# Scores of two slots in one burst, and the first projection in items of 2x256 tokens with the odd tokens of four batches together

One core of one Trainium2 chip. The metric is the device time of one execution in microseconds; the core's span in the trace is some 1.8 us shorter.

## The reference

Attention of 8 batches x 8 heads x 576 tokens x 64 in which only scores within tau of the row's maximum count, followed by two projections with a gate between them.

```python
scores = scale * np.matmul(q, k.transpose(0, 1, 3, 2))
thresh = np.max(scores, axis=-1, keepdims=True) - tau
scores = np.where(scores >= thresh, scores, -1000000000.0)
attn = np.exp(scores - np.max(scores, axis=-1, keepdims=True))
attn = attn / (np.sum(attn, axis=-1, keepdims=True) + 1e-09)
x = np.matmul(attn, v)            # to (4608 tokens, 512)
h = x @ w_in                      # 512 -> 2048
g = h * np.clip(h + 3.0, 0.0, 6.0) / 6.0
return g @ w_out                  # 2048 -> 512
```

## The kernel before

The work is cut into 144 slots: 128 query rows of two heads, nine slots for four heads (a "quad"), 18 for a batch. In the traces here each engine executes its instructions in program order. A slot goes through the engines like this: scores on TensorE (PE) into PSUM; two copies with maximum on VectorE (DVE), "the maxima"; a bias on GpSimd (POOL); mask and exponential on ScalarE (ACT); reciprocal on DVE; normalising on POOL; transposing by DMA. Projections of an earlier batch are laid between: an "item" of the first projection (eight matmuls, a ReLU on ACT or DVE, a gate on DVE) and a "quarter" of a second-projection tile (four matmuls; after the fourth quarter DVE evicts the tile).

```python
for n, sl in enumerate(queue):
    ...                                     # exp of the slot before (ACT)
    sm_max(sl)                              # two maxima on DVE, then bias on POOL
    if slot != 8 and todo1:
        item, then = todo1.pop(0)
        h = mm1(item)                       # PE, in ps_h: two banks, one buffer
        r = mm1_relu(h, on_act=(slot in (0, 1, 3, 5)))
        mm1_gate(item, h, r)                # DVE
        ...
    ...                                     # reciprocal of the slot before (DVE)
    for _ in range(pieces):                 # one quarter in most slots
        if todo2:
            mm2_part(bb, mt, part)
            if part == 3:
                outs += mm2_out(bb, mt, on_act=False)   # eviction, DVE
    for i in range(2):
        sm_mask(sl, i)
    ...                                     # one job: a transpose, or attention x V
    if n + 1 < len(queue):
        queue[n + 1].tiles = scores(queue[n + 1].quad, queue[n + 1].slot)
    ...
# after the loop: the rest of the projections, with PSUM of the scores as well
```

A slot's scores fill four banks, and there is one such set: the next slot's scores wait for this slot's maxima.

## Time and profile before

| | before |
|---|---|
| median, us | 560.3 |
| span in the trace, us | 558.7 |
| start of slot 22's scores | 74.7 |
| start of slot 142's scores | 495.0 |
| from there to the end | 63.7 |
| a slot, mean of 120 | 3.50 |

From slot 22 on the projections run within the loop; the stretch up to slot 142 is the steady part, and what comes after it is called the end below. The page, the groups, the chain and the timeline of before are shown in the prediction.

### The profile page before, as it was taken

The numbers are of one execution on the slowest core, as the hardware profiler recorded it, in microseconds if no ns is written. First come the engines' busy times: TensorE is split into PE (matmuls) and PEld (weight loads), VectorE is DVE, ScalarE is ACT, GpSimd is POOL, SyncE is SP. The second block draws the span as 40 slices with busy tenths as digits, with TensorE's granted clock in tenths as the row PEclk, the third lists the DMA queues.
The fourth block names the chain that finished last, engine by engine and source line by source line (L and its number), as shares of the span: only waits on it lengthen the run. The fifth ranks groups of instructions, "written<-read, shape, count | busy, mean of one in ns | idle before, by whom it ended". The sixth has DMA issues, their size and how long they took to land.

```text
span 558.7 us, 11624 instructions
## 1 busy us (share of the span) xinstructions
PE 530.6 (95%) x3829; PEld 309.2 (55%) x3870; DVE 424.7 (76%) x1041; ACT 469.7 (84%) x999; POOL 305.3 (55%) x646
## 2 busy tenths in 40 slices
PE   8899798799999999999999999999999999999997
PEld 6655455555555555655555555655555565654663
DVE  3787686787878788887978788887978798883440
ACT  4899899798889999899898999899898999984440
POOL 2788878854556555755556555755556555561000
PEclk9999899999999999999999999999999999999999
DMA  5999979976789869978689889977689865454102
GB/s 121 137 120 173 196 128 190 204 142 126 137 158 152 152 136 157 178 149 146 130 148 152 173 131 160 175 147 147 131 145 166 150 144 114 100 109 94 38 20 76
DMA packets 286348, 77.52 MB, mean 139 GB/s; under 512 B 269264, under 2 KB 281808, under 8 KB 286288
## 3 DMA queue, kind: packets, MB, share of 16 engines
q1 hardware_dynamic: 267680, 67.47, 65.3%
q0 software_dynamic: 17408, 8.92, 13.6%
q8 instruction: 30, 0.49, 0.4%
q10 hardware_dynamic: 1200, 0.39, 0.3%
q14 instruction: 30, 0.25, 0.1%
HBM read 36.70 MB, written 9.44 MB: 83 GB/s over the span
## 4 chain that ended last, share of the span: by engine, by line
PE 55%; DVE 11%; ACT 8%; issue 4%; SPq 3%; DMA 2%; POOL 2%; DVEq 0%; POOLq 0%
PE h L357 17%; PE o L386 16%; PE s L260 15%; DVE s L281 5%; PE av L327 3%; ACT s L289 3%; ACT s L294 3%; DMA nq<-in_q_dram 2%; DVE g L374 2%; DVE r L368 2%; ACT r L366 1%; PE s L266 1%; PE tp L214 1%; SPq L310 1%; POOL pn L302 1%
## 5 line engine op out<-in xcount | busy, mean ns | idle before, releaser
L302 POOL TENSOR_SCALAR pn<-s,rinv 128x576 bf16<-128x576 f32 x288 | 211.6, 745 | 133.1 <-DVE rinv L297 57.3
L289 ACT ACTIVATE s<-s,bias 128x576 f32<-128x576 f32 x288 | 206.9, 766 | 36.3 <-POOL bias L284 35.2
L281 DVE TENSOR_SCALAR_CACHE_REDUCE s<-s 128x576 f32<-128x576 f32 x288 | 205.9, 752 | 40.3 <-PE s L260 29.9
L294 ACT ACTIVATE s<-s 128x576 f32<-128x576 f32 x288 | 192.7, 671 | 0.3
L260 PE MATMUL s<-kT,qT 64*128 64x288 f32 x1024 | 169.7, 430 | 5.1 <-DVE s L281 2.8
L357 PE MATMUL h<-xT,w_in_sb 128*128 128x320 bf16 (+1 forms) x1024 | 144.9, 287 | 5.9 <-DVE g L374 5.0
L386 PE MATMUL o<-w_out_sb,g 128*128 128x512 bf16 x535 | 133.5, 379 | 5.2 <-DVE osb L394 3.0
L357 PEld LDWEIGHTS <-w_in_sb 128*128 128x128 bf16 x1024 | 92.1, 97 | 68.9 <-issue 31.9
L374 DVE SCALAR_TENSOR_TENSOR g<-r,h 128x512 bf16<-128x512 f32 (+1 forms) x128 | 96.4, 755 | 41.7 <-ACT r L366 39.9
L260 PEld LDWEIGHTS s<-kT,qT 64*128 64x128 f32 x1024 | 93.7, 186 | 60.9 <-DVE s L281 24.0
L284 POOL TENSOR_SCALAR bias<-m 128x1 f32<-128x1 f32 x288 | 54.4, 189 | 66.6 <-DVE s L281 45.8
L386 PEld LDWEIGHTS <-g 128*128 128x128 bf16 x576 | 55.6, 98 | 57.4 <-issue 9.0
L366 ACT ACTIVATE r<-h,three 128x640 f32<-128x640 f32 (+1 forms) x74 | 54.4, 736 | 20.6 <-PE h L357 19.9
L294 ACT ACTIVATION_READ_ACCUMULATOR s<-s 128x1 f32 x288 | 54.2, 188 | 0.0
L368 DVE TENSOR_SCALAR r<-h 128x512 f32<-128x512 f32 (+1 forms) x54 | 40.5, 751 | 0.0
L394 DVE TENSOR_SCALAR osb<-o 128x512 f32<-128x512 f32 x31 | 21.0, 676 | 21.4 <-PE o L386 21.4
L327 PE MATMUL av<-pT,vm 128*64 128x512 bf16 x256 | 34.6, 393 | 2.0 <-ACT kT L204 2.0
L327 PEld LDWEIGHTS <-vm 128*64 128x64 bf16 x512 | 18.0, 111 | 25.3 <-issue 18.8
L297 DVE RECIPROCAL rinv<-rsum 128x2 f32<-128x2 f32 x144 | 23.0, 160 | 11.3 <-ACT s L294 10.5
L339 DVE CAST xT<-av 128x512 bf16<-128x512 f32 x32 | 21.8, 681 | 6.6 <-PE av L330 6.3
L281 DVE DVE_READ_ACCUMULATOR s<-s 128x1 f32 x288 | 23.9, 83 | 0.0
L266 PE MATMUL s<-kT,qT 64*64 64x288 f32 x256 | 20.1, 415 | 0.7 <-DVE s L281 0.7
(44 smaller groups left out, 241.4 us busy)
## 6 DMA issues: line engine op xcount, KB each, us to landing
km<-in_k_dram SPq DMA_DIRECT2D x64, 128.0 KB, 3.0
out_dram<-osb SPq DMA_DIRECT2D x31, 256.0 KB, 2.4
nq<-in_q_dram SPq DMA_DIRECT2D x96, 72.0 KB, 2.7
vm<-in_v_dram POOLq DMA_DIRECT2D x16, 256.0 KB, 5.6
w_in_sb<-in_moe_w_in_dram POOLq DMA_DIRECT2D x16, 128.0 KB, 4.3
w_out_sb<-in_moe_w_out_dram POOLq DMA_DIRECT2D x16, 128.0 KB, 4.5
pT<-pn SPq DMA_TRANSPOSE x119, 3.4
nq<-in_q_dram SPq DMA_DIRECT2D x14, 128.0 KB, 4.4
```

The source lines that it names most:

```text
L260: nc.tensor.matmul(tiles[a][:, hf, 0:HALF], qT_of(pair)[a * 64:(a + 1) * 64, t * P:(t + 1) * P], keys(pair, a, hf), start=True, stop=True)
L281: nc.vector.tensor_scalar(out=sl.s[:, i, :].rearrange("p (a b) -> p a b", a=2), in0=ps[:, :, 0:HALF], scalar1=1.0, scalar2=None, op0=Alu.m ...
L284: nc.gpsimd.tensor_scalar(out=sl.bias[:, i:i + 1], in0=sl.m[:, i:i + 1], scalar1=-scale, scalar2=tau, op0=Alu.mult, op1=Alu.add)
L289: nc.scalar.activation(out=s, in_=s, func=Act.Prelu, bias=sl.bias[:, i:i + 1], scale=scale, alpha=REJECT)
L294: nc.scalar.activation(out=s, in_=s, func=Act.Exp, accum_out=sl.rsum[:, i:i + 1])
L302: nc.gpsimd.tensor_scalar(out=pn[:, i, :], in0=sl.s[:, i, :], scalar1=sl.rinv[:, i:i + 1], scalar2=1.0, op0=Alu.mult, op1=Alu.mult)
L327: nc.tensor.matmul(ps[a * 64:(a + 1) * 64, :], vm[:, 2 * hp + a, c * D:(c + 1) * D], pT[:, 5 * a + c, cols], start=(c == 0), stop=False)
L357: nc.tensor.matmul(hps[:, n, 0:w], w_in_sb[:, ki, (ni + n) * P:(ni + n + 1) * P], xT[b][:, ki, c0:c0 + w], start=(ki == 0), stop=(ki == KI ...
L366: nc.scalar.activation(out=r, in_=hps, func=Act.Relu, bias=three[:])
L368: nc.vector.tensor_scalar(out=r, in0=hps, scalar1=3.0, scalar2=0.0, op0=Alu.add, op1=Alu.max)
L374: nc.vector.scalar_tensor_tensor(out=gbuf[:, ni:ni + 2, c0:c0 + w], in0=r, scalar=6.0, in1=hps, op0=Alu.min, op1=Alu.mult)
L386: nc.tensor.matmul(o_ps[0], gbuf[:, ni, mt * P:(mt + 1) * P], w_out_sb[:, ni, :], start=(ni == 0), stop=(ni == NI - 1))
```

## The change

The intent, as I read the code, is to spare PE the switch between the scores (fp32, 64-row tiles of the array) and the projections (bf16, the whole array) in every other slot. PSUM holds the scores of two slots in six banks; the even slot's tile has a large part (384 columns) in a bank of its own and a small part (192) in a bank that it shares with the odd slot. The attention products and transposes borrow the even slot's two large banks after its maxima. To make room, the first projection gets one bank (2x256 in place of up to 2x320), so the 64 odd tokens of each batch are collected for four batches. Quarters come two at a time in even slots; jobs that end on DVE come in odd slots.

```diff
+    def score_tile(n, a, rows=slice(0, P), k0=0, w=S):
+        c0 = 1536 * (1 - a) + (128 if lower(n) else 832) + k0
+        return ps_flat[rows, c0:c0 + w]
...
+    def scores(*ns):
+        parts = [(n, small) for n in reversed(ns) for small in (True, False)]
+        if len(ns) == 2 and all(n % NSLOT != 8 for n in ns):
+            parts.insert(0, parts.pop(2))
+        for n, small in parts:
+            score_part(n, small)
...
-        if slot != 8 and todo1:
-            item, then = todo1.pop(0)
+        if todo1 or todo3:
+            item, then = (todo1 or todo3).pop(0)
             h = mm1(item)
-            r = mm1_relu(h, on_act=(slot in (0, 1, 3, 5)))
+            r = mm1_relu(h, on_act=n % 2 == 0)
...
-        for _ in range(pieces):
+        for _ in range(0 if n % 2 else 2):
             if todo2:
...
+        elif quad % 2:
+            jobs = {0: ["q1", "av0late"], 1: ["k1"], 4: ["av1", "avr"], 5: ["alloc", "k0"], 6: ["q0"], 7: ["rest"],
+                    8: ["av0"]}
+        else:
+            jobs = {1: ["q1"], 2: ["k1"], 3: ["av1", "avr"], 4: ["alloc", "k0"], 5: ["q0"], 6: ["rest"]}
...
-        if n + 1 < len(queue):
-            queue[n + 1].tiles = scores(queue[n + 1].quad, queue[n + 1].slot)
+        if n + 1 < N1:
+            scores(n + 1)
+        elif n % 2 and n + 2 < len(queue):
+            scores(n + 1, n + 2)
```

More of the change, by code (lines that the diff above doesn't have):

```diff
@@ L43 @@
     N1 = 22
-    N2 = 28
+    HB = 6
+    OB = 7
     scale = 1.0 / math.sqrt(D)
+    M = 2 * 512
     tau = float(tau)
@@ L60 @@
     o_pool = ctx.enter_context(tc.tile_pool(name="op", bufs=3))
-    ps_s = ctx.enter_context(tc.psum_pool(name="ps_s", bufs=2))
-    ps_h = ctx.enter_context(tc.psum_pool(name="ps_h", bufs=1))
-    ps_o = ctx.enter_context(tc.psum_pool(name="ps_o", bufs=1))
-    ps_m = ctx.enter_context(tc.psum_pool(name="ps_m", bufs=1))
+    ps_pool = ctx.enter_context(tc.psum_pool(name="ps", bufs=1))
     ctx.enter_context(tc.manual_schedule())
+    ps = ps_pool.tile([P, 8, 512], F32, name="ps")
+    ps_flat = ps[:].rearrange("p b c -> p (b c)")
     nat = {}
@@ L73 @@
     xT = {}
+    xR = {}
     loads = []
@@ L162, in warm_up @@
     def warm_up(count):
-        warm = ps_h.tile([P, 2, 512], F32, tag="h", name="warm")
         for _ in range(count):
-            nc.tensor.transpose(warm[:, 0, 0:P], identf[:], identf[:])
+            nc.tensor.transpose(ps[:, 6, 0:P], identf[:], identf[:])
     warm_up(14)
@@ L171 @@
     nc.vector.memset(three[:], 3.0)
-    gbuf = g_pool.tile([P, NI, 2 * S], BF16, name="g")
+    gbuf = g_pool.tile([P, NI, M + 256], BF16, name="g")
     def alloc_qk(quad):
@@ L190, with burst, bank @@
     turn = 0
-    def bank(name):
+    def burst(n):
+        return n >= N1
+    def bank():
         nonlocal turn
         turn += 1
-        if now < N2 and turn % 2:
-            return ps_o.tile([P, 512], F32, tag="o", name=name)
-        return ps_m.tile([P, 512], F32, tag="m", name=name)
+        return ps[:, ((3, 0) if now < N1 else (5, 2))[turn % 2], :]
     def copy_out(out, in_):
@@ L208, in by_pe, with main_pe, transpose_q @@
         return pair // NPAIR < NB
-    def main_pe(src, pair):
-        ps = bank("tp")
+    def main_pe(src, pair, pb=None):
+        pb = bank() if pb is None else pb
         n = pair % 2
         for t in range(4):
-            nc.tensor.transpose(ps[:, t * P:(t + 1) * P], src[:, t, 2 * n:2 * n + 2, :], identf[:])
-        return ps
-    def transpose_q(pair):
+            nc.tensor.transpose(pb[:, t * P:(t + 1) * P], src[:, t, 2 * n:2 * n + 2, :], identf[:])
+        return pb
+    def transpose_q(pair, pb=None):
         nq = nat[pair // 2][0]
         if by_pe(pair):
-            ps = main_pe(nq[:, 0:1024].rearrange("p (t h d) -> p t h d", h=4, t=4), pair)
-            return lambda: nc.vector.tensor_copy(out=qT_of(pair)[:, 0:512], in_=ps[:])
+            pb = main_pe(nq[:, 0:1024].rearrange("p (t h d) -> p t h d", h=4, t=4), pair, pb)
+            return lambda: nc.vector.tensor_copy(out=qT_of(pair)[:, 0:512], in_=pb)
         n = pair % 2
         nc.vector.transpose(out=qT_of(pair), in_=nq[:, n * S:(n + 1) * S])
+        return lambda: None
     def transpose_k(pair):
-        ps = main_pe(nat[pair // 2][1], pair)
-        return lambda: copy_out(kT_of(pair)[:, 64:576], ps[:])
+        pb = main_pe(nat[pair // 2][1], pair)
+        return lambda: copy_out(kT_of(pair)[:, 64:576], pb)
     def transpose_rest(quad, of_k=True, of_q=True):
-        ps = bank("tr")
+        pb = bank()
         nq, _, kr = nat[quad]
@@ L233, in transpose_rest @@
         if of_k:
-            nc.tensor.transpose(ps[:, 0:P], kr[:], identf[:])
+            nc.tensor.transpose(pb[:, 0:P], kr[:], identf[:])
         if of_q:
-            nc.tensor.transpose(ps[:, P:2 * P], nq[:, 1024:1152], identf[:])
+            nc.tensor.transpose(pb[:, P:2 * P], nq[:, 1024:1152], identf[:])
         def evict():
             qT, kT = qkT[quad]
-            both = ps[:].rearrange("p (w n t) -> p w n t", n=2, t=64)
+            both = pb.rearrange("p (w n t) -> p w n t", n=2, t=64)
             if of_q:
@@ L246, in transpose_rest, with keys @@
         return evict
-    def keys(pair, a, hf):
-        kT = kT_of(pair)
-        c0 = 64 * (1 - a) + hf * HALF
-        return kT[a * 64:(a + 1) * 64, c0:c0 + HALF]
-    def scores(quad, slot):
-        tiles = [ps_s.tile([P, 2, 512], F32, tag="s", name="s") for _ in range(2)]
-        for hf in range(2):
-            if slot < 8:
-                pair, t = 2 * quad + slot // 4, slot % 4
-                for a in range(2):
-                    nc.tensor.matmul(tiles[a][:, hf, 0:HALF], qT_of(pair)[a * 64:(a + 1) * 64, t * P:(t + 1) * P],
-                                     keys(pair, a, hf), start=True, stop=True)
-            else:
-                for n in range(2):
-                    for a in range(2):
-                        pair = 2 * quad + n
-                        nc.tensor.matmul(tiles[a][n * 64:(n + 1) * 64, hf, 0:HALF],
-                                         qT_of(pair)[a * 64:(a + 1) * 64, 512:S], keys(pair, a, hf),
-                                         start=True, stop=True)
-        return tiles
+    def keys(pair, a, k0, w):
+        c0 = 64 * (1 - a) + k0
+        return kT_of(pair)[a * 64:(a + 1) * 64, c0:c0 + w]
@@ new lines, in score_tile, with lower, score_part @@
+    def score_tile(n, a, rows=slice(0, P), k0=0, w=S):
+        c0 = 1536 * (1 - a) + (128 if lower(n) else 832) + k0
+        return ps_flat[rows, c0:c0 + w]
+    def lower(n):
+        return burst(n) and n % 2
+    def score_part(n, small):
+        quad, slot = divmod(n, NSLOT)
+        k0, w = ((384, 192) if small else (0, 384)) if lower(n) else ((0, 192) if small else (192, 384))
+        if slot < 8:
+            pair, t = 2 * quad + slot // 4, slot % 4
+            for a in range(2):
+                nc.tensor.matmul(score_tile(n, a, k0=k0, w=w), qT_of(pair)[a * 64:(a + 1) * 64, t * P:(t + 1) * P],
+                                 keys(pair, a, k0, w), start=True, stop=True)
+        else:
+            for i in range(2):
+                for a in range(2):
+                    pair = 2 * quad + i
+                    nc.tensor.matmul(score_tile(n, a, rows=slice(i * 64, (i + 1) * 64), k0=k0, w=w),
+                                     qT_of(pair)[a * 64:(a + 1) * 64, 512:S], keys(pair, a, k0, w),
+                                     start=True, stop=True)
@@ L279, in sm_max @@
         sl.rinv = stat_pool.tile([P, 2], F32, tag="rinv", name="rinv")
-        for i, ps in enumerate(sl.tiles):
-            nc.vector.tensor_scalar(out=sl.s[:, i, :].rearrange("p (a b) -> p a b", a=2), in0=ps[:, :, 0:HALF],
+        for i in range(2):
+            nc.vector.tensor_scalar(out=sl.s[:, i, :], in0=score_tile(sl.n, i),
                                     scalar1=1.0, scalar2=None, op0=Alu.mult, op1=Alu.max,
@@ L313, in pe_transpose, with av @@
     def pe_transpose(sl):
-        ps = ps_h.tile([P, 2, 1024], BF16, tag="h", name="pt")
-        ps = ps[:].rearrange("p a b -> p (a b)")[:, 0:2 * S].rearrange("p (c t) -> p c t", t=P)
+        pb = ps_flat[:, 3072:3072 + S].bitcast(BF16).rearrange("p (c t) -> p c t", t=P)
         pn = sl.pn[:].rearrange("p a b -> p (a b)")
         for c in range(9):
-            nc.tensor.transpose(ps[:, c, :], pn[:, c * P:(c + 1) * P], identb[:])
-        return lambda: nc.vector.tensor_copy(out=sl.dst, in_=ps)
-    def av(ps, pair, pT, cols):
+            nc.tensor.transpose(pb[:, c, :], pn[:, c * P:(c + 1) * P], identb[:])
+        return lambda: nc.vector.tensor_copy(out=sl.dst, in_=pb)
+    def av(pb, pair, pT, cols):
         b, hp = divmod(pair, NPAIR)
@@ L326, in av @@
             for a in range(2):
-                nc.tensor.matmul(ps[a * 64:(a + 1) * 64, :], vm[:, 2 * hp + a, c * D:(c + 1) * D],
+                nc.tensor.matmul(pb[a * 64:(a + 1) * 64, :], vm[:, 2 * hp + a, c * D:(c + 1) * D],
                                  pT[:, 5 * a + c, cols], start=(c == 0), stop=False)
         for a in range(2):
-            nc.tensor.matmul(ps[a * 64:(a + 1) * 64, :], vr[:, a, hp, :], pT[:, 4, cols], start=False, stop=True)
+            nc.tensor.matmul(pb[a * 64:(a + 1) * 64, :], vr[:, a, hp, :], pT[:, 4, cols], start=False, stop=True)
     def av_main(pair):
@@ L334, in av_main, with mm1 @@
         if hp == 0:
-            xT[b] = x_pool.tile([P, KI, S], BF16, tag="xT", name="xT")
-        ps = bank("av")
-        av(ps[:], pair, pts[pair], slice(0, 512))
-        o0 = 64 if b % 2 else 0
-        nc.vector.tensor_copy(out=xT[b][:, hp, o0:o0 + 512], in_=ps[:])
+            xT[b] = x_pool.tile([P, KI, 512], BF16, tag="xT", name="xT")
+        pb = bank()
+        av(pb, pair, pts[pair], slice(0, 512))
+        nc.vector.tensor_copy(out=xT[b][:, hp, :], in_=pb)
     def av_rest(quad):
         b, g = divmod(quad, 2)
-        ps = bank("ar")
+        pb = bank()
         for n in range(2):
-            av(ps[:, n * 64:(n + 1) * 64], 2 * quad + n, ptr[quad], slice(n * 64, (n + 1) * 64))
-        o0 = 0 if b % 2 else 512
-        nc.vector.tensor_copy(out=xT[b][:, 2 * g:2 * g + 2, o0:o0 + 64],
-                              in_=ps[:, 0:P].rearrange("p (a b) -> p a b", a=2))
-    def mm1(item, pool=None):
-        b, ni, c0, w = item
-        hps = (pool or ps_h).tile([P, 2, 512], F32, tag="s" if pool else "h", name="h")
+            av(pb[:, n * 64:(n + 1) * 64], 2 * quad + n, ptr[quad], slice(n * 64, (n + 1) * 64))
+        if b % 4 == 0 and g == 0:
+            xR[b // 4] = x_pool.tile([P, KI, 256], BF16, tag="xR", name="xR")
+        o0 = 64 * (3 - b % 4)
+        nc.vector.tensor_copy(out=xR[b // 4][:, 2 * g:2 * g + 2, o0:o0 + 64],
+                              in_=pb[:, 0:P].rearrange("p (a b) -> p a b", a=2))
+    def mm1(item, hb=HB):
+        src, ni, c0, _ = item
+        hps = ps[:, hb, :].rearrange("p (n w) -> p n w", n=2)
         for n in range(2):
             for ki in range(KI):
-                nc.tensor.matmul(hps[:, n, 0:w], w_in_sb[:, ki, (ni + n) * P:(ni + n + 1) * P],
-                                 xT[b][:, ki, c0:c0 + w], start=(ki == 0), stop=(ki == KI - 1))
-        return hps[:, :, 0:w]
+                nc.tensor.matmul(hps[:, n, :], w_in_sb[:, ki, (ni + n) * P:(ni + n + 1) * P],
+                                 src[:, ki, c0:c0 + 256], start=(ki == 0), stop=(ki == KI - 1))
+        return hps
     def mm1_relu(hps, on_act):
-        w = hps.shape[2]
-        r = r_pool.tile([P, 2, 320], F32, tag="r", name="r")[:, :, 0:w]
+        r = r_pool.tile([P, 2, 256], F32, tag="r", name="r")[:]
         if on_act:
@@ L371, in mm1_gate, with mm2_part, mm2_out @@
     def mm1_gate(item, hps, r):
-        b, ni, c0, w = item
-        c0 += (b % 2) * S
-        nc.vector.scalar_tensor_tensor(out=gbuf[:, ni:ni + 2, c0:c0 + w], in0=r, scalar=6.0, in1=hps,
+        _, ni, _, g0 = item
+        nc.vector.scalar_tensor_tensor(out=gbuf[:, ni:ni + 2, g0:g0 + 256], in0=r, scalar=6.0, in1=hps,
                                        op0=Alu.min, op1=Alu.mult)
     o_ps = {}
-    def mm2_part(bb, mt, part, pool=None):
+    def mm2_part(b, t, part, ob=OB):
+        g0 = M + 64 * (3 - b % 4) if t == 4 else 512 * (b % 2) + P * t
         if part == 0:
-            if pool:
-                o_ps[0] = pool.tile([P, 2, 512], F32, tag="s", name="o")[:, 0, :]
-            else:
-                o_ps[0] = ps_o.tile([P, d_model], F32, tag="o", name="o")[:]
+            o_ps[0] = ps[:, ob, :]
         for ni in range(part * 4, part * 4 + 4):
-            nc.tensor.matmul(o_ps[0], gbuf[:, ni, mt * P:(mt + 1) * P], w_out_sb[:, ni, :],
+            nc.tensor.matmul(o_ps[0], gbuf[:, ni, g0:g0 + P], w_out_sb[:, ni, :],
                              start=(ni == 0), stop=(ni == NI - 1))
-    def mm2_out(bb, mt, on_act):
+    def mm2_out(b, t, on_act):
         osb = o_pool.tile([P, d_model], F32, tag="osb", name="osb")
@@ L394, in mm2_out @@
             nc.vector.tensor_scalar_mul(out=osb[:], in0=o_ps[0], scalar1=1.0 / 6.0)
-        b0 = 2 * bb * S
-        if mt == 4:
-            return [(osb[0:64, :], out[b0 + 512:b0 + S, :]), (osb[64:P, :], out[b0 + S + 512:b0 + 2 * S, :])]
-        r0, t = (b0, mt) if mt < 4 else (b0 + S, mt - 5)
-        return [(osb[:], out[r0 + t * P:r0 + (t + 1) * P, :])]
+        r0 = b * S + t * P
+        if t == 4:
+            return [(osb[0:64, :], out[r0:r0 + 64, :]), (osb[64:P, :], out[r0 - S:r0 - S + 64, :])]
+        return [(osb[:], out[r0:r0 + P, :])]
     todo1 = []
+    todo3 = []
     todo2 = []
@@ L412, in moe_of, with moe_of_rest @@
         items = []
-        for c0, w, mts in (((0, 320, (4, 5, 6)), (320, 256, (7, 8))) if b % 2 else
-                           ((0, 256, (0, 1)), (256, 320, (2, 3)))):
+        for c0 in (0, 256):
             for ni in range(0, NI, 2):
-                items.append(((b, ni, c0, w), ()))
-            items[-1] = (items[-1][0], [(b // 2, mt, part) for mt in mts for part in range(4)])
+                items.append(((xT[b], ni, c0, 512 * (b % 2) + c0), ()))
+            items[-1] = (items[-1][0], [(b, t, part) for t in (c0 // P, c0 // P + 1) for part in range(4)])
+        return items
+    def moe_of_rest(b):
+        items = [((xR[b // 4], ni, 0, M), ()) for ni in range(0, NI, 2)]
+        items[-1] = (items[-1][0], [(c, 4, part) for c in (b, b - 2) for part in range(4)])
         return items
@@ L432 @@
             sl = Slot()
-            sl.quad, sl.slot = quad, slot
+            sl.quad, sl.slot, sl.n = quad, slot, len(queue)
             sl.on_chip = len(queue) < N1 - 1 and len(queue) % 2 == 1
             queue.append(sl)
-    queue[0].tiles = scores(0, 0)
+    scores(0)
+    plan = []
+    for sl in queue:
+        quad, slot = sl.quad, sl.slot
+        if sl.n < N1:
+            jobs = {1 if quad else 2: ["q1"], 2 if quad else 3: ["k1"], 5: ["alloc", "q0"], 6: ["k0"], 7: ["rest"],
+                    8: ["av0"]}
+            if quad == 0:
+                jobs[1] = ["rest0"]
+            else:
+                jobs[3], jobs[4] = (["av1"], ["avr"]) if quad == 1 else (["av1", "avr"], [])
+        elif quad % 2:
+            jobs = {0: ["q1", "av0late"], 1: ["k1"], 4: ["av1", "avr"], 5: ["alloc", "k0"], 6: ["q0"], 7: ["rest"],
+                    8: ["av0"]}
+        else:
+            jobs = {1: ["q1"], 2: ["k1"], 3: ["av1", "avr"], 4: ["alloc", "k0"], 5: ["q0"], 6: ["rest"]}
+        if quad + 1 == NQUAD:
+            jobs = {s: [j for j in jobs[s] if j not in ("alloc", "k0", "q0", "rest")] for s in jobs}
+        plan.append(jobs.get(slot, []))
     prev = None
@@ L469 @@
         outs = []
-        pieces = 0 if slot == 3 else 1
-        if slot == 0:
-            second = True
-        if second and slot < 2 and len(todo2) > 1 and todo2[0][1] == todo2[1][1]:
-            pieces, second = 2, False
-        for _ in range(pieces):
+        for _ in range(0 if n % 2 else 2):
             if todo2:
-                bb, mt, part = todo2.pop(0)
-                mm2_part(bb, mt, part)
+                b2, t2, part = todo2.pop(0)
+                mm2_part(b2, t2, part)
@@ L481 @@
                 if part == 3:
-                    outs += mm2_out(bb, mt, on_act=False)
+                    outs += mm2_out(b2, t2, on_act=False)
         for i in range(2):
             sm_mask(sl, i)
-        evict = None
         nxt = 2 * quad + 2
-        if slot == (1 if quad else 2):
-            evict = transpose_q(2 * quad + 1)
-        elif slot == (2 if quad else 3):
-            evict = transpose_k(2 * quad + 1)
-        elif n == 1:
-            evict = transpose_rest(0, of_k=False)
-        elif slot == 3 and quad > 0:
-            av_main(2 * quad - 1)
-        elif slot == 4 and quad > 0:
-            av_rest(quad - 1)
-            if quad % 2 == 0:
-                todo1.extend(moe_of(quad // 2 - 1))
-        elif slot in (5, 6, 7) and quad + 1 < NQUAD:
-            if slot == 5:
-                alloc_qk(quad + 1)
-                evict = transpose_q(nxt)
-            elif slot == 6:
-                evict = transpose_k(nxt)
-            else:
-                evict = transpose_rest(quad + 1)
-        elif slot == 8:
-            av_main(2 * quad)
@@ L509 @@
-        if evict:
-            evict()
+        for job in plan[n]:
+            if job == "alloc":
+                alloc_qk(quad + 1)
+            elif job == "q1":
+                transpose_q(2 * quad + 1)()
+            elif job == "k1":
+                transpose_k(2 * quad + 1)()
+            elif job == "q0":
+                transpose_q(nxt)()
+            elif job == "k0":
+                transpose_k(nxt)()
+            elif job == "rest":
+                transpose_rest(quad + 1)()
+            elif job == "rest0":
+                transpose_rest(0, of_k=False)()
+            elif job == "av1":
+                av_main(2 * quad - 1)
+            elif job == "av0":
+                av_main(2 * quad)
+            elif job == "av0late":
+                av_main(2 * quad - 2)
+            elif job == "avr":
+                av_rest(quad - 1)
+                if quad % 2 == 0:
+                    todo1.extend(moe_of(quad // 2 - 1))
+                if quad % 8 == 0:
+                    todo3.extend(moe_of_rest(quad // 2 - 1))
@@ L534 @@
     last = NQUAD - 1
-    count = [1, 0]
+    count = [0, 0]
     def last_out():
@@ L546, in rest1 @@
     def rest1(item, then):
-        h = mm1(item, pool=ps_s if count[0] % 3 else None)
+        h = mm1(item, hb=count[0] % 6)
         count[0] += 1
@@ L553, in rest2 @@
         while todo2:
-            bb, mt, part = todo2.pop(0)
-            mm2_part(bb, mt, part, pool=ps_s if count[1] % 3 else None)
+            b2, t2, part = todo2.pop(0)
+            mm2_part(b2, t2, part, ob=6 + count[1] % 2)
             if part == 3:
                 flush()
-                if (bb, mt) == (B // 2 - 1, 8):
+                if (b2, t2) == (B - 1, 3):
                     last_out()
                 else:
-                    late.extend(mm2_out(bb, mt, on_act=(count[1] % 2 == 0)))
+                    late.extend(mm2_out(b2, t2, on_act=(count[1] % 2 == 0)))
                 count[1] += 1
-    for item in todo1:
+    for item in todo1 + todo3:
         rest1(*item)
@@ L568 @@
     av_rest(last)
-    for item in moe_of(B - 1):
+    for item in moe_of_rest(B - 1) + moe_of(B - 1):
         rest1(*item)
```

## The prediction

> **What bounds the kernel now.** I read the page first, then the groups by shape, then the chain of the work that ended last between 300 and 345 us, then the timeline of the same place.
>
> ```profile
> PE 530.6 (95%) x3829; PEld 309.2 (55%) x3870; DVE 424.7 (76%) x1041; ACT 469.7 (84%) x999; POOL 305.3 (55%) x646
> ...
> PE 55%; DVE 11%; ACT 8%; issue 4%; SPq 3%; DMA 2%; POOL 2%; DVEq 0%; POOLq 0%
> ```
>
> TensorE is busy 95% and holds 55% of the chain. Busy is not streaming, so I looked at a stretch of the chain (start us, us, what):
>
> ```profile
> 316.07 0.98 PE h L357 x8
> 317.05 0.05 issue
> 317.10 1.67 PE o L386 x7
> 318.77 1.17 PE s L260 x8
> 319.94 0.98 PE h L357 x8
> 320.92 0.86 PE o L386 x4
> 321.79 1.17 PE s L260 x8
> 322.96 0.98 PE h L357 x8
> ```
>
> A plain slot is scores 1.17, a 256-wide projection item 0.98, one quarter of a second-projection tile 0.86: 3.02 us with no wait, PE alone. Adding per 18 slots (one batch) 18 x 1.17 + 16 items x 1.085 (mean of 0.98 and 1.19) + 18 x 0.86 + four attention products of 1.19 + two small ones of 0.45 + four key transposes of 0.44 + two of 0.22 gives 61.8 us, or 3.43 a slot. Score starts in the trace, from slot 22 (74.7 us) to slot 142 (495.0 us), are 3.50 apart, and 3.49 in the later half. So the loop is TensorE bound with under 2% of waiting. After the last slot come some 60 us of projections alone.
>
> What the other engines do in a slot (busy us, mean ns of one):
>
> ```profile
> L281 DVE TENSOR_SCALAR_CACHE_REDUCE s<-s 128x576 f32<-128x576 f32 x288 | 205.9, 752 | 40.3 <-PE s L260 29.9 <-issue 3.0 <-POOL bias L284 2.6
> ...
> L374 DVE SCALAR_TENSOR_TENSOR g<-r,h 128x512 bf16<-128x512 f32 x64 | 44.0, 688 | 18.8 <-ACT r L366 17.9
> ...
> L366 ACT ACTIVATE r<-h,three 128x512 f32<-128x512 f32 x36 | 24.5, 682 | 5.2 <-PE h L357 5.0
> ...
> L394 DVE TENSOR_SCALAR osb<-o 128x512 f32<-128x512 f32 x31 | 21.0, 676 | 21.4 <-PE o L386 21.4
> ```
>
> Back to back these overlap by some 0.08 each: the timeline has the maxima 0.68 apart, and the gate's successor 0.60 after it. ACT needs about 3.1 us a slot, DVE 2.9.
>
> ```profile
> 303.33 0.75 DVE L281 TENSOR_SCALAR_CACHE_REDUCE s<-s 128x576 f32<-128x576 f32 x1
> ...
> 304.01 0.08 DVE L281 DVE_READ_ACCUMULATOR s<-s 128x1 f32 x1
> ...
> 304.29 0.79 PEld L260 LDWEIGHTS s<-kT,qT 64*128 64x128 f32 x8 [0.42 <-DVE s L281]
> 304.30 1.24 PE L260 MATMUL s<-kT,qT 64*128 64x288 f32 x8
> ```
>
> The last maximum ends at 304.09 and the next scores start 0.20 later: the hand-over that the change makes longer or shorter.
>
> **What the Trainium skill says.** "Trainium Kernel Development and Optimization", Performance Expectations: matmul busy time is a bad measure of distance from the roofline, as matmuls are pipelined. Agreed here: of the 3.02 us of a plain slot 2.70 stream. "TensorE: Matmul & The Clock Gate", Back-to-back issue gap: N/2.4 + 2.5 ns, so 109 and 216 ns at 256 and 512 columns; single records here start 108.5 and 216 ns apart. The same page, What happens when you issue a matmul: only weight loads are pulled ahead, matmuls stay in program order, so one waiting score matmul holds all behind it. The waits in this trace agree. "PSUM — Partial Sum Buffer", PSUM bank collisions: accesses are to be guarded by bank and quadrant, not by address. The built program agrees: the burst's first 192-wide matmul, which shares only a bank with the slot before, carries a wait on DVE.
>
> **The change, part by part.**
>
> *Removed on PE.* In single records a score group of four pass pairs starts at 304.295, its passes 0.242 apart, and the projection's first matmul starts at 305.563: 1.27, of which 0.97 streams, 0.105 is the first weight load and 0.195 the switch back. A burst of two slots pays the 0.30 once: 1.94 + 0.30 = 2.24 against 2.54. That is 0.15 a slot, or 18 us in 121 slots. The split into 192 and 384 columns streams as long as 288 twice. Projection columns are the same in number (144 items of 256 for 128 of 256 or 320), and each item's DVE work too.
>
> *Moved.* One pair of slots on PE is burst 2.24, item 0.87, two quarters 1.73, item 0.87 = 5.71 plus the jobs of that pair (0 to 2.09; 7.9 in nine pairs). If PE alone counted, nine pairs would take about 57.5 us against 62.8 measured for 18 slots now.
>
> *Added: a longer loop through DVE.* The order of instructions says that a burst waits for the odd slot's maxima, and on DVE there stand between burst and these: the even slot's maxima, its gate, a reciprocal, and in every second pair an output eviction. From the burst's start: its last matmul ends at 2.21 (drain 0.16 as recorded), maxima from 2.28 to 3.64; the item ends at 3.27, its ReLU on ACT runs 3.30 to 3.98, so the gate runs 4.00 to 4.60; reciprocal to 4.68; the odd maxima to 6.11 (0.68 + 0.75); hand-over 0.20: the next burst not before **6.33**. With an eviction: the two quarters stream until 4.84 and drain at 5.00, eviction 5.05 to 5.65, maxima to 7.08, next burst not before **7.28**. PE's 5.71 lies inside both; only pairs with many PE jobs outlast them.
>
> Nine pairs, by first slot modulo 18, the larger of PE and DVE; 0, 4, 8, 14 evict:
> 0: 7.28 (PE 5.71); 2: 7.80 (PE, keys and both attention products); 4: 7.28; 6: 6.33; 8: 7.28; 10: 6.33 (no second projection there); 12: 7.36 (PE); 14: 7.28; 16: 7.12 (PE). Sum 64.1, and about 1.2 more after pair 8, where the q transpose and the attention copy come after the odd gate on DVE and hold the burst's last part, which needs their bank. 65.3 for 18 slots, 3.63 a slot; about 1.7 less per batch before slot 76, where pair 2 has no items. Over slots 22 to 142 that is 427 us against 420.3 now: **+7**, although PE's own work shrank.
>
> *The end.* In the new order 30 items and 44 quarters follow the last burst; now it is 21 items and 34 quarters after the last scores. From slot 142's scores to the end: burst 2.2, 240 matmuls x 0.1087 = 26.1, 176 x 0.2165 = 38.1, attention 2.9, waits (last transposes, ReLU and gate) about 3, last eviction and store 4.1 = 76.4 against 558.7 - 495.0 = 63.7 now: **+12.7**. Less streams in the loop in exchange, but that only widens PE's waits if DVE's loop sets the pace.
>
> Sum: 560.5 + 7 + 12.7 = 580. Waits that I left out would add; pairs in which I have laid two waits in a row that in fact overlap would take off. I put 578.
>
> **The rivals.**
> 1. *PE stays the bound.* Loop 120 slots at about 3.15 to 3.2 and 12.7 more at the end: about 530 to 537. For it: PE is the bound now, and jobs were placed with care (DVE jobs only in odd slots, behind the burst). Against it: in six of nine pairs PE's own work is 0.4 to 1.9 us shorter than the DVE chain, and program order lets PE do nothing else meanwhile.
> 2. *DVE's loop, but evictions and the ReLU wait fall mostly beside PE-bound pairs*, about 3.5 a slot: the loop as now, the end longer: 570.
> 3. *ACT joins.* Its work per pair is 6.2, with a key copy 6.7, above 6.33; masks wait for a bias that stands behind two normalisations on POOL. If the ReLU then comes late, each pair grows by 0.2 to 0.4: 590.
> 4. *DMA.* Its share is 0.82 to 0.92 in the loop now; a loop no faster asks no more of it. I give it little.
>
> **Range and chances.** Rivals 2 and 3 bound the mechanism at 570 and 590. Rival 1, and the chance that someone who placed jobs so carefully had measured a gain, I give a sixth; it stretches the low side. 578, range 550 to 592. Faster by over 2% (below 549) 0.15, within 2% (to 572) 0.20, slower 0.65.
>
> **What would show it.** Right: score bursts of about 2.2 us, with idle time of PE or its weight load before their first matmul put down to the maxima on DVE, tens of us in total (24 + 2.8 now); idle time of DVE before the even maxima put down to scores; bursts 7.2 to 7.4 us apart where an eviction lies between, 6.3 to 6.5 in pairs without much PE work; PE's busy share in the loop below 93%; slot 142's scores near 502 us and 76 us after them. Wrong: bursts 5.7 to 6.2 us apart in pairs without jobs, which means that the maxima do not wait for the whole burst or that evictions come later; or a projection phase at the end of about 60 us.

## The result

| | before | after | predicted |
|---|---|---|---|
| median, us | 560.3 (559.6 to 561.2, 4 runs) | 581.7 (580.5 to 582.0, 4 runs) | 578 |
| ratio to before | | 1.0377 (1.0363 to 1.0392) | |
| slot 142's scores at | 495.0 | 502.7 | 502 |
| slots 22 to 142 | 420.3 | 428.1 | 427 |
| from there to the end | 63.7 | 77.6 | 76.4 |

The page after, busy time and the chain:

```profile
PE 535.2 (92%) x3998; PEld 328.2 (57%) x3998; DVE 424.2 (73%) x1060; ACT 473.6 (82%) x1012; POOL 305.3 (53%) x646
...
PE 45%; ACT 15%; DVE 13%; issue 7%; POOL 4%; DMA 3%; DVEq 0%; POOLq 0%
```

Only the weight loads got more work worth naming (PEld 309.2 to 328.2 us, off the bound); the share of every other engine fell, and PE holds 45% of the chain in place of 55%. The loop from 200 to 490 us, before and then after (us, then busy of PE, weight loads, DVE, ACT, POOL):

```profile
sum 290.00, PE 285.14 PEld 164.20 DVE 242.64 ACT 266.59 POOL 164.72; mean PE 95.05 PEld 54.73 DVE 80.88 ACT 88.86 POOL 54.91
```

```profile
sum 290.00, PE 274.69 PEld 168.25 DVE 233.05 ACT 259.24 POOL 160.77; mean PE 91.56 PEld 56.08 DVE 77.68 ACT 86.41 POOL 53.59
```

PE goes from 98.3% to 94.7%, and DVE, ACT and POOL are idler as well: a loop of waits, not a full engine. A pair with an eviction (slots 126 and 127, pair 0 of the table below) in the timeline after (start us, us, engine, line, operation; L269 scores, L372 and L397 projections, L380 ReLU, L296 maxima, L387 gate, L405 eviction):

```profile
446.36 2.21 PE L269 MATMUL ps<-kT,qT 64*128 64x192 f32 x16
...
448.50 1.05 PE L372 MATMUL ps<-xT,w_in_sb 128*128 128x256 bf16 x8
448.69 0.76 DVE L296 TENSOR_SCALAR_CACHE_REDUCE s<-ps 128x576 f32<-128x576 f32 x1 [1.33 <-PE ps L269]
...
449.38 1.89 PE L397 MATMUL ps<-w_out_sb,g 128*128 128x512 bf16 x8
...
449.58 0.69 ACT L380 ACTIVATE r<-ps,three 128x512 f32<-128x512 f32 x1 [0.47 <-PE ps L372]
...
450.31 0.69 DVE L387 SCALAR_TENSOR_TENSOR g<-r,ps 128x512 bf16<-128x512 f32 x1 [0.17 <-ACT r L380]
...
451.11 1.04 PE L372 MATMUL ps<-xT,w_in_sb 128*128 128x256 bf16 x8
451.31 0.69 DVE L405 TENSOR_SCALAR osb<-ps 128x512 f32<-128x512 f32 x1 [0.24 <-PE ps L397]
...
451.92 0.74 DVE L296 TENSOR_SCALAR_CACHE_REDUCE s<-ps 128x576 f32<-128x576 f32 x1
...
452.59 0.75 DVE L296 TENSOR_SCALAR_CACHE_REDUCE s<-ps 128x576 f32<-128x576 f32 x1
452.73 0.29 PEld L269 LDWEIGHTS ps<-kT,qT 64*128 64x128 f32 x2 [0.86 <-DVE s L296]
452.73 2.88 PE L269 MATMUL ps<-kT,qT 64*128 64x192 f32 x16 [0.58 <-DVE s L296]
```

The first burst takes 2.21 us and DVE stands idle for 1.33 us until it ends. Then the chain runs as the prediction has it: even maxima, gate behind ACT's ReLU, eviction behind the two quarters, odd maxima, and only then the next burst. The second burst shows how such waiting hides: from its first to its last matmul it takes 2.88 us, because the row half whose maximum was done at 452.7 starts and the other half starts 0.68 us later, one maximum. For 0.59 us of that time two matmuls of the first half alone count as PE busy, and only 0.09 us is idle. So I compare pairs by the start of the last matmul of each burst.

| pair (first slot modulo 18) | 0 | 2 | 4 | 6 | 8 | 10 | 12 | 14 | 16 | sum |
|---|---|---|---|---|---|---|---|---|---|---|
| predicted | 7.28 | 7.80 | 7.28 | 6.33 | 8.48 | 6.33 | 7.36 | 7.28 | 7.12 | 65.3 |
| after, median of 3 to 7 | 7.04 | 7.67 | 7.05 | 6.26 | 8.40 | 6.10 | 7.97 | 7.21 | 7.03 | 64.7 |

(The 8.48 holds the 1.2 us that the prediction put behind pair 8; pair 2 is taken from slot 92 on, where it has items.)

The end. The chain before, and then after (start us, us, what):

```profile
509.44 10.74 PE o L386 x49
...
521.65 15.72 PE h L357 x126
...
537.63 10.74 PE o L386 x49
...
548.42 6.22 PE o L386 x28
```

```profile
512.63 3.20 DMA pT<-pn
...
519.75 13.97 PE ps L397 x64
...
534.55 20.90 PE ps L372 x190
555.45 20.73 PE ps L397 x96
```

In these long pieces PE streams with hardly a gap before and after, only there is more left to do: 24 items in a row for 16, and 160 second-projection matmuls for 126 in these lines. After also waits 3.2 us for the last transposes, as predicted.

### The profile page after: what moved, and what is told of

It is laid out like the page before. It is cut to its first block, busy times and chain, and to the rows that moved or that the text cites. A ratio compares the mean times of both kernels' runs of the same rounds, so it can differ in the third digit from the quotient of the medians.

```text
span 580.2 us, 12005 instructions
## 1 busy us (share of the span) xinstructions
PE 535.2 (92%) x3998; PEld 328.2 (57%) x3998; DVE 424.2 (73%) x1060; ACT 473.6 (82%) x1012; POOL 305.3 (53%) x646
## 4 chain that ended last, share of the span: by engine, by line
PE 45%; ACT 15%; DVE 13%; issue 7%; POOL 4%; DMA 3%; DVEq 0%; POOLq 0%
PE ps L397 14%; PE ps L372 13%; PE ps L269 13%; DVE s L296 7%; ACT s L304 6%; ACT s L309 5%; ACT r L380 3%; PE ps L341 3%; POOL pn L317 3%; DMA w_out_sb<-in_moe_w_out_dram 2%; DVE g L387 1%; PE ps L275 1%; DVE r L382 1%; DVE xT L352 1%; DMA pR<-pn 1%
## 5 line engine op out<-in xcount | busy, mean ns | idle before, releaser
L296 DVE TENSOR_SCALAR_CACHE_REDUCE s<-ps 128x576 f32<-128x576 f32 x288 | 206.1, 751 | 58.3 <-PE ps L269 42.8
L269 PE MATMUL ps<-kT,qT 64*128 64x192 f32 (+1 forms) x1024 | 170.5, 424 | 11.7 <-DVE s L296 5.1
L372 PEld LDWEIGHTS <-w_in_sb 128*128 128x128 bf16 x1152 | 107.6, 98 | 69.2 <-issue 54.0
L372 PE MATMUL ps<-xT,w_in_sb 128*128 128x256 bf16 x1024 | 130.6, 273 | 16.0 <-DVE g L387 15.3
L397 PE MATMUL ps<-w_out_sb,g 128*128 128x512 bf16 x576 | 133.3, 379 | 1.5 <-DMA w_out_sb<-in_moe_w_out_dram 0.8
L269 PEld LDWEIGHTS ps<-kT,qT 64*128 64x128 f32 x1024 | 96.2, 186 | 57.9 <-DVE s L296 24.6
L387 DVE SCALAR_TENSOR_TENSOR g<-r,ps 128x512 bf16<-128x512 f32 x144 | 98.8, 687 | 37.2 <-ACT r L380 35.1
L397 PEld LDWEIGHTS <-g 128*128 128x128 bf16 x576 | 56.0, 98 | 59.5 <-issue 3.0
L380 ACT ACTIVATE r<-ps,three 128x512 f32<-128x512 f32 x86 | 58.7, 685 | 34.4 <-PE ps L372 33.8
L405 DVE TENSOR_SCALAR osb<-ps 128x512 f32<-128x512 f32 x30 | 20.6, 688 | 31.9 <-PE ps L397 31.9
L382 DVE TENSOR_SCALAR r<-ps 128x512 f32<-128x512 f32 x58 | 39.8, 686 | 0.6 <-PE ps L372 0.6
L341 PE MATMUL ps<-pT,vm 128*64 128x512 bf16 x256 | 34.6, 393 | 1.8 <-DMA pT<-pn 1.8
L275 PE MATMUL ps<-kT,qT 64*64 64x384 f32 (+1 forms) x256 | 23.4, 417 | 3.3 <-DVE s L296 1.3
```

What stands on the lines that cost most here:

```text
L269: nc.tensor.matmul(score_tile(n, a, k0=k0, w=w), qT_of(pair)[a * 64:(a + 1) * 64, t * P:(t + 1) * P], keys(pair, a, k0, w), start=True, st ...
L296: nc.vector.tensor_scalar(out=sl.s[:, i, :], in0=score_tile(sl.n, i), scalar1=1.0, scalar2=None, op0=Alu.mult, op1=Alu.max, accum_out=sl.m ...
L341: nc.tensor.matmul(pb[a * 64:(a + 1) * 64, :], vm[:, 2 * hp + a, c * D:(c + 1) * D], pT[:, 5 * a + c, cols], start=(c == 0), stop=False)
L372: nc.tensor.matmul(hps[:, n, :], w_in_sb[:, ki, (ni + n) * P:(ni + n + 1) * P], src[:, ki, c0:c0 + 256], start=(ki == 0), stop=(ki == KI - 1))
L380: nc.scalar.activation(out=r, in_=hps, func=Act.Relu, bias=three[:])
L382: nc.vector.tensor_scalar(out=r, in0=hps, scalar1=3.0, scalar2=0.0, op0=Alu.add, op1=Alu.max)
```

## The experiments

Names in bold are the runs' labels. "Loop" is the time from the last matmul of slot 22's scores (their burst, where there are bursts) to that of slot 142's: 420.3 before, 428.9 after.

**a_late_evict.** The eviction is held back until the odd maxima are issued.

```diff
+    held = []
...
         sm_max(sl)
+        outs = []
+        if held:
+            outs += mm2_out(*held.pop(), on_act=False)
...
-        outs = []
...
-                    outs += mm2_out(b2, t2, on_act=False)
+                    held.append((b2, t2))
```

> Only the output eviction on DVE moves: from between the even slot's gate and the odd slot's maxima to just behind the odd maxima. Theory (a burst waits for the odd maxima, and all that stands ahead of them on DVE is on the path): the four eviction pairs of nine fall from 7.04 us between burst ends to about 6.5, so 27 x 0.5 = 13 us less, 564 to 572 us in all. Rival (ACT's own work, or a bias late on POOL, sets the pace of the pairs): the same work in another order, at most 3 us less, 578 to 583.

Measured: 568.8 us, ratio 1.0143; loop 417.5. As expected. The eviction pairs 0, 4 and 14 went from 7.04, 7.05 and 7.21 to 6.10, 6.16 and 6.32; pair 8 stayed at 8.40, and pairs 6 and 16 grew by 0.48 and 0.14, which I did not trace. Timeline of pair 0 in this run (L405 eviction, L382 the odd slot's ReLU):

```profile
442.25 0.73 DVE L296 TENSOR_SCALAR_CACHE_REDUCE s<-ps 128x576 f32<-128x576 f32 x1
...
442.91 0.75 DVE L296 TENSOR_SCALAR_CACHE_REDUCE s<-ps 128x576 f32<-128x576 f32 x1
443.35 2.59 PE L269 MATMUL ps<-kT,qT 64*128 64x192 f32 x16
...
443.59 0.68 DVE L405 TENSOR_SCALAR osb<-ps 128x512 f32<-128x512 f32 x1
...
444.19 0.68 DVE L382 TENSOR_SCALAR r<-ps 128x512 f32<-128x512 f32 x1
```

The same work, moved behind the maxima, lies beside the burst. So the place of the eviction cost 11.4 us of loop, net of what pairs 6 and 16 lost: shown.

**b_single.** Bursts off, everything else as changed.

```diff
-        return n >= N1
+        return False
...
-        return ps[:, ((3, 0) if now < N1 else (5, 2))[turn % 2], :]
+        return ps[:, (3, 0)[turn % 2], :]
...
-        if n + 1 < N1:
-            scores(n + 1)
-        elif n % 2 and n + 2 < len(queue):
-            scores(n + 1, n + 2)
+        if n + 1 < len(queue):
+            scores(n + 1)
```

> The bursts alone are undone: one slot's scores at a time again, with the new projection items, the new jobs and the new places of the second projection kept. Theory: a score group then waits for one slot's maxima only and PE is the bound again: 57.5 + 9 x 0.3 = 60.2 us of PE work per 18 slots and a little waiting, about 3.4 a slot, 408 us for 120 slots, with 75 before and 77.5 behind: 558 to 566 us. Rival (the loss comes from the one bank of the projection, or from the second projection in even slots only): stays at 576 to 584.

Measured: 580.2 us, ratio 1.0345; loop 426.5. A miss: undoing the bursts alone gave nothing back. Its chain shows why (start us, us, what):

```profile
447.06 1.22 PE ps L269 x8
...
448.35 0.19 DVE s L296
...
449.04 0.76 DVE s L296 x3
449.80 0.61 DVE r L382
...
450.43 0.70 DVE g L387
...
451.18 1.03 PE ps L372 x8
```

After the odd slot's scores (447.06) PE has one item, but the chain goes through DVE: the odd maxima, for which the next scores wait, then the odd slot's ReLU and gate, for which the next item waits, since it needs the projection's one bank. The two waits end together: in the timeline those scores start at 449.17, are held up halfway for the second maximum and end at 451.08. With both quarters in even slots there is too little PE work in odd ones to cover 1.45 us of maxima.

**b2_single_quarter.** b_single with one quarter in every slot.

```diff
-        for _ in range(0 if n % 2 else 2):
+        for _ in range(1):
```

> As the run with one slot's scores at a time, which stayed at 580, but with one quarter of a second-projection tile in every slot in place of two in even slots. My explanation of that miss: with both quarters in even slots PE has only one item of 0.87 us (and jobs) between the odd slot's scores and the next ones, which wait for 1.45 us of odd maxima, and an eviction stands ahead of these, so DVE's chain paced there too. Then this run is PE bound, about 3.4 us a slot, 406 to 413 us for 120 slots, 558 to 565 in all. Rival (items of 256 in one bank, and the rest tokens of four batches together, cost the time): stays at 574 to 582.

Measured: 564.8 us, ratio 1.0075; loop 410.9, then 76.6 to the end. As expected: the new items in one bank, the rest tokens of four batches together and the new jobs cost under 1% in all: the loop is 9.4 us shorter than before, the end 12.9 us longer. Bursts, with both quarters in even slots, cost 18 us of loop on top (428.9 against 410.9). With one slot's scores at a time the quarters' place alone costs 15.6 of it (426.5 against 410.9), and bursts then add 2.3. Bursts with one quarter in every slot were not run, so what bursts alone cost stays open.

**c_relu_swap.** The even ReLU on DVE, the odd one on ACT.

```diff
-            r = mm1_relu(h, on_act=n % 2 == 0)
+            r = mm1_relu(h, on_act=n % 2 == 1)
```

> ReLU of even items on DVE and of odd ones on ACT, so as many as before on each, but now the even one stands ahead of the odd maxima on DVE: gate from 4.39 in place of 4.00 us after the burst's start. Theory: 0.39 x about 40 pairs that DVE's chain paces, 594 to 602 us. Rival (throughput of ACT or of DVE paces): no work is added, 579 to 585.

Measured: 592.7 us, ratio 1.0570; loop 439.0, so 10.1 more with no work added. A little less than expected: in pairs 0 and 10 nothing changed (7.04 and 6.11), in pairs 4, 6 and 14 it added 0.12 to 0.22, and nearly all of it fell on pairs 16 (0.88) and 2 (0.56), which the prediction had put down to PE. In an eviction pair the later gate can hide in the wait for the quarters (0.24 us idle ahead of the eviction above). In pair 16 the trace shows another path than the odd maxima: the odd gate now waits for ACT, the attention copy stands behind it, and the burst that begins at 387.84 waits in its last part for that copy's bank:

```profile
388.33 0.69 DVE L387 SCALAR_TENSOR_TENSOR g<-r,ps 128x512 bf16<-128x512 f32 x1 [1.29 <-ACT r L380]
...
389.01 0.67 DVE L352 CAST xT<-ps 128x512 bf16<-128x512 f32 x1
...
389.74 0.29 PEld L269 LDWEIGHTS ps<-kT,qT 64*128 64x128 f32 x2 [0.31 <-DVE xT L352]
```

This burst spans 2.81 us where in the changed kernel it spans 2.21: 0.60 of the 0.88. Pair 2 I did not trace. So the run speaks against throughput as the pace, as no work was added, but it is no proof of the step through the odd maxima.

**g_dve_extra** and **h_act_extra.** One idle instruction more in each even slot from 22 on, on one engine. In the trace of g_dve_extra the memset takes 272 ns, in that of h_act_extra the copy 284 ns (285 in the trace of k_f1_act_extra), 61 of each.

```diff
+        if n >= N1 and n % 2 == 0:
+            nc.vector.memset(scratch[:], 0.0)          # g_dve_extra, ahead of the masks
         for i in range(2):
             sm_mask(sl, i)
+        if n >= N1 and n % 2 == 0:
+            nc.scalar.copy(out=scratch2[:], in_=scratch[:])   # h_act_extra
```

> A memset of 128x256 on DVE (some 0.2 us of pace) is added in even slots from 22 on, ahead of the odd maxima: 61 times. Theory (DVE's chain paces six of nine pairs): 0.2 x 40 = 8, so 587 to 593 us. Rival (ACT or PE paces): 580 to 584.

> A copy of 128x128 on ACT (some 0.2 to 0.25 us of pace) is added behind the masks of even slots from 22 on, 61 times, with nothing else changed. Theory (DVE's chain paces; ACT has 6.2 us of work in a pair of 7.1): at most 3 us more, 581 to 585 us. Rival (ACT paces, as its 90% of the loop and its 15% of the chain say): 0.22 x 61 = 13, so 593 to 597 us.

Measured: 590.5 us (ratio 1.0529) with DVE's, 584.2 us (ratio 1.0411) with ACT's. The profiled execution of h_act_extra took 2881 us; the three others, 583.2 to 584.3, are used, and nothing is read from its timeline but the copy's length. Nearly equal work costs 8.8 us on DVE ahead of the odd maxima and 2.4 us on ACT. The trace of g_dve_extra says where: pairs 0, 4, 6, 8, 10 and 14, the six in which the prediction had DVE's chain outlast PE, grew by 0.22 or 0.23 each, pairs 2 and 16 not at all, and pair 12 fell by 0.17. So DVE's chain paces these six, and ACT, though 15% of the chain, hardly does.

**d_even_first.** Where the odd slot before a burst used neither of the two large banks, the burst starts with the even slot.

```diff
+        if len(ns) == 2 and free_banks(ns[0] - 1):
+            parts = [(ns[0], False), (ns[0], True), (ns[1], True), (ns[1], False)]
...
```

> The burst's order alone changes where the odd slot before it left the two big score banks free (five of nine pairs): the even slot's large part first, which needs no maxima of the odd slot, then its small part, then the odd slot. The even maxima can then begin about 1 us earlier. Theory: pairs behind such a burst lose 0.7 to 1.0 us, 33 of them, so 549 to 560 us. Rival (the score matmuls' waiting is not what paces): 576 to 583.

Measured: 575.2 us, ratio 1.0261; loop 420.8. A miss: just below the rival's range and far from the theory's. The direction is right, the size (8.0 us of loop) about a third of what I expected: pairs 0, 4 and 14 lost 0.65, pair 10 0.33 and pair 6 0.14, but pairs 8 and 12 grew by 0.35.

**e_both.** a_late_evict and d_even_first together.

> Both mends together: output eviction behind the odd maxima, and the even slot first in the burst where its banks are free. Theory: most pairs come near PE's own work, 3.25 to 3.35 us a slot, 390 to 402 us for 120 slots, and with 75 before and 77.5 behind 543 to 555 us, faster than both kernels. Rival: not below 565.

Measured: 570.0 us, ratio 1.0171; loop 417.1. A miss, the rival's range: with the late eviction the even-first order adds nothing (417.5 without it). What pairs 0, 6 and 10 gain, pairs 8 and 12 lose again.

**f1_late_av_first.** a_late_evict, and the attention copy ahead of the q transpose in pair 8.

```diff
-            jobs = {0: ["q1", "av0late"], 1: ["k1"],
+            jobs = {0: ["av0late", "q1"], 1: ["k1"],
```

> The run with the late eviction, and in pair 8 of nine the attention copy on DVE ahead of the q transpose, so that the bank which the burst's last part needs is free some 0.7 us earlier. Theory (that pair's 8.4 us in place of 7.3 comes from this order): 0.7 x 6 or 7 = 4 to 5 us off 568.8, so 563 to 566. Rival (something else, such as V's loads issued on POOL there, makes the pair long): 567 to 570.

Measured: 565.5 us, ratio 1.0079; loop 412.3. As expected. Pair 8 went from 8.40 to 7.74 and no other pair moved by over 0.01: the order of two DVE instructions, through a bank, is worth 5.2 us of loop.

**f2_all_swap.** e_both, the attention copy first and the ReLUs swapped.

> Late eviction, even slot first in the burst where it can be, attention copy first, and the even ReLU on DVE with the odd one on ACT. With both mends the trace shows the even gate waiting 1 to 2.4 us for ACT's ReLU, which stands behind two exponentials, so ACT's order has become what paces. If so this goes to 552 to 562 us. If DVE's own chain still paces, the swap adds as it did alone, and it stays at 568 to 580.

Measured: 580.9 us, ratio 1.0349; loop 427.4. The reading that ACT's order had become what paces falls: the loop is 10.3 longer than in e_both, though the attention copy comes first. What the swap costs here by itself no run shows; if the copy's place is worth 5.2 as in f1_late_av_first, it is more than the 10.1 that it cost alone.

**k_f1_act_extra** and **l_f1_dve_extra.** The idle instructions of above on top of f1_late_av_first.

> The copy of 0.284 us on ACT in 61 even slots, now on top of the kernel with the late eviction and the attention copy first (565.5 us). Where it was added to the changed kernel it cost 2.4 us. My guess of what paces after the mend: ACT, whose own work per pair (6.2 us) is now close to the pair's 6.1 to 6.7. If so, 8 to 14 us more, 573 to 580. If PE or DVE's chain paces there too: 565 to 569.

> The memset of 0.272 us on DVE in 61 even slots, on top of the same mended kernel. In the changed kernel it cost 8.8 us. If ACT paces after the mend, at most 4 us, 565 to 569; if DVE's chain still does, 572 to 576.

Measured: 567.0 us (ratio 1.0122) with ACT's, 572.1 us (ratio 1.0202) with DVE's; f1_late_av_first has 1.0079. My guess fell again: ACT's costs 0.4%, DVE's 1.2%. By pairs (medians, as in the table), DVE's adds 0.17 to 0.23 in pairs 0, 4, 10 and 14, 0.06 in pair 6 and nothing in 2, 8 and 16; ACT's adds 0.19 in pair 8 and 0.02 or less elsewhere. After both mends DVE's chain still sets the pace of four of nine pairs; there the 0.30 us of switching that a burst saves on PE cannot show. No version beat the kernel before.

## Why the prediction was right

**The bound before** held: PE busy for 98% of the loop.

**The loop.** Predicted +7 us, measured +7.8. The step that carries it, "a burst waits for the odd slot's maxima, and on DVE there stand ... its gate, a reciprocal, and in every second pair an output eviction", is shown by two runs that shorten or lengthen just that chain: eviction taken off it (0.9 us less in pairs 0, 4 and 14, 11.4 us of loop), a memset of 0.27 us put on it (0.22 more in each of the six pairs that the prediction gave to DVE, 8.8 us in all). The swapped ReLUs (+10.1) are no third proof: they cost most in two other pairs. The nine pair times agree within 0.24 us, but for one.

**The sum** is nearer than its parts. Six batches of 65.3, pairs 4 to 14 once more (43.1) and three times 1.7 off give 430 us, not the recorded 427: +9.5, not +7. The parts were some 0.6 a batch too long, so that the loop's agreement within 1 us is in part luck. (By its own steps 6.33 should read 6.31.)

**That one is pair 12**: 7.36 predicted as PE's own work, 7.97 in four of seven cases, 8.39 and 9.05 in two. In the chain a load of V issued on POOL comes ahead of the bias; these lines are of the case of 8.39, and the same order stands in the cases of 7.97:

```profile
424.42 0.70 POOL vm L125
...
425.31 0.19 POOL bias L299
...
425.53 1.44 ACT s L304 x2
```

That is the third rival's mechanism, a bias late on POOL, in one pair of nine. The chain goes on through mask, exponential, ReLU and gate to the odd item, which needs the projection's one bank and waits for the gate, some 0.57 us in the cases of 7.97 and 1.00 in that of 8.39: a path that the prediction did not have. The seventh case, slot 138, lies in the last batch, where no V is left to load, and took 7.44. No run moved that load, so this points to it and does not show it.

**Pair 8's 1.2 us**, "the q transpose and the attention copy come after the odd gate on DVE and hold the burst's last part", is right: exchanging the two gave 0.66 us of it back, with the late eviction in place.

**The end.** Predicted +12.7 us, measured +13.8: 30 items and 44 quarters behind the last burst for 21 and 34, by the order of the instructions, at the same rate of streaming (second projection: 10.74 us for 49 matmuls before, 13.97 for 64 after). Behind slot 142's first score PE was busy for 70.7 us in place of 58.3; these 12.4 us of PE work left the loop and did not make it shorter.

**What was off.** PE's busy share was to fall "below 93%" in the loop; it is 94.7%, in part because one row half's matmuls count as busy while the other half waits (0.59 us in the burst above), and the waits of the score's weight loads for the maxima grew only from 26.8 to 32.9 us in all. Bursts "7.2 to 7.4 us apart where an eviction lies between" come near for the ends of bursts (7.04 to 7.21, pair 8 apart), not for their starts (6.37), as one row half starts a maximum early; "6.3 to 6.5 in pairs without much PE work" came out as 6.26 and 6.10. That early start was not in my hand-over of 0.20 us; the pairs paced by DVE came out 0.07 to 0.24 us too long.

**A point that the prediction did not make**: it laid the loss on the burst. b_single shows that the single-slot form loses as much with the quarters where they are; what the two have in common, by their chains, is that between two groups of scores PE has less work than DVE's chain takes. b2_single_quarter bears this out for the single-slot form; for bursts the like run is missing.

## What to carry to other kernels

Before grouping work on the engine that bounds, add up the in-order chain on the others between one group's end and the next one's start: grouping halves the switches, but puts two slots' worth of steps, and whatever stands between them in program order, into one wait. Instructions that only free a buffer (an eviction, a copy) belong behind the one that releases the bounding engine. And count what a shorter loop leaves for the end: work that is pushed out of a loop which waits is paid in full.

## What the Trainium skill lacked or had wrong

- "TensorEngine Tiling (Array Packing)", Key Properties, says that changing the tiling mode drains the engine and gives no figure. Here a group of 64-row fp32 scores between full-array bf16 matmuls costs 0.195 us on leaving and, where its first weight load is not hidden, 0.105 us on entry (trace of before, from 304.295); a burst of two slots that waits for nothing takes 2.14 us from its start to the next projection's, for 1.94 us of streaming.
- "TensorE: Matmul & The Clock Gate", Back-to-back issue gap, gives a sustained 131 ns a matmul at 512 columns in a stream of loads and matmuls. The same section's N/2.4 + 2.5, which it gives for single matmuls, 216 ns, is what the runs show: 96 in 20.73 us at the end.
- "Trainium Kernel Development and Optimization", Performance Expectations, says that matmul busy time is a bad measure of the roofline; no page says that of two row tiles one can wait unseen while the other's matmuls count as busy. Here a burst of 2.21 us spans 2.88 us where one row half starts 0.68 us late, and only 0.09 us of that shows as idle.
